# Raw attention outputs of chunks 0 and 1 in a buffer of their own, and four early steps of VectorE and ScalarE in another order

## The chip, the cores and the metric

The kernel runs on one core of a Trainium2 chip. The metric is the device time of one execution in microseconds (us); lower is better. TensorE (PE) does the matmuls, VectorE (DVE) and ScalarE (ACT) the elementwise work, GpSimd (POOL) a few small steps, and SyncE (SP) issues nearly all DMAs. Each engine works through its own list of instructions in order; semaphores make one engine wait for another or for a DMA.

## The reference

```python
# retention over 768 tokens, 4 batches, 8 heads, head size 64
for t in range(S):
    state = gamma * state + outer(k[:, :, t], v[:, :, t])
    y[:, :, t] = scale * (q[:, :, t] @ state)
x = y.transpose(0, 2, 1, 3).reshape(3072, 512)
# then a gated layer
h = x @ w_in                  # 512 -> 2048
g = h * sigmoid(h)
out = g @ w_out               # 2048 -> 512
```

All is float32 at the interface. The weights arrive in 64-bit form and are turned into float32 words on the chip.

## The kernel before, in words

**Tiling.** The 768 tokens are cut into 6 chunks of 128. A *unit* is one chunk of one batch, so there are 24 units; unit n is chunk n // 4 of batch n % 4. `w_in` is cut into 16 slices of 128 columns. A *product* (c, f) is chunk c of all four batches (512 rows) times slice f. Each operand of a large matmul is split into three parts (high, low and third), so a product is 8 matmuls into PSUM tile `ha` (4 with the high part of x, then 4 with the low part) and 4 into `hb` (third part). After all products a second stage multiplies g by `w_out`.

**One unit in attention.** `stage_t` (L436, L438) turns k and q over on TensorE (tiles kp and qp) and ScalarE copies them out (kt, qt). `scale_k`, written K (L398), scales k. TensorE then computes sc (L452, L462). `steps_a`, written A three times, makes am on VectorE (L470), mid (L476 on ScalarE in chunk 0, L478 on VectorE later) and the new state (L482). `scale_q`, written Q (L403), scales qt. `stage_y` computes y in PSUM in three groups (L501): the scores part from am, the first half of the states part from qt with mid and state, and the second half behind a fence on GpSimd (L377). The PSUM tile of y has one buffer, so the scores of unit n + 1 wait until unit n's y has been copied out.

**From y to x.** `steps_y`, written X four times, takes y on. The first step is the *raw copy* on ScalarE (L539) from PSUM to SBUF, for chunks up to `LATE` = 2. The second is the high part of x on ScalarE (L552), then the low part (L555) and the third part (L558), both on VectorE. The raw copy goes to a tile of pool `hpool`, tag "hs", which has three buffers. The same three buffers hold the results g of the products: `close_steps` copies `ha` out (L655, ScalarE), subtracts `hb` (L660, VectorE), applies silu (L665, ScalarE), and `put_g` stores the tile with a DMA on SyncE (L671). A buffer comes free when its put has landed or its last reader is done.

**Weights.** `early_slice`, written W, turns slices 0 to 2 of `w_in` into float32 (L196 on ScalarE, L199 to L217 on VectorE) and splits them (L120, L126 on ScalarE; L123, L128 on VectorE), one step at each call.

**What sets the order.** TensorE's order is that of the program throughout. Until L874 the order of SyncE, VectorE, ScalarE and GpSimd is also the written one: the lines from L763 to L873 are a schedule made by hand, in which units 0 to 7, the weight slices 0 to 2 and the first four products (P(0), P(1), P(2) and P(NF), which are products 0 to 2 of chunk 0 and product 0 of chunk 1) interleave. After that a scheduler orders these engines from given constraints. The part that the change touches lies wholly in the first 70 us. The tag "wq" in pool `wpool` holds 24 KB per partition: first chunk 2's x (units 8 to 11), later four weight slices.

Of the kernel before, what the change touches and what calls it, by code (L numbers as in the profile page):

```python
# [13 lines left out]
FP32 = mybir.dt.float32  # L14
# [19 lines left out]
def kernel(  # L34
# [28 lines left out]
    nc = tc.nc  # L63
    B, H, S, D = q.shape
    DM, DF = moe_w_in.shape
    C = 128
    NC = S // C
    HP = H // 2
    KIN = DM // 128
# [11 lines left out]
    def pool(name, bufs, **kw):  # L81
        return ctx.enter_context(tc.tile_pool(name=name, bufs=bufs, **kw))

    dram = pool("dram", 1, space=bass.MemoryType.DRAM)
    wpool = pool("wpool", 1)
# [12 lines left out]
    y_dram = [dram.tile([128, KIN, C], FP32, tag=f"y{b}", name=f"yd_{b}") for b in range(B)]  # L98
# [136 lines left out]
    def early_slice(i):  # L235

        out = []
        yield from convert_steps(i, out)
        yield
        steps = split_steps(i, out[0], "wi", scale, w_sb, None)  # L240
        next(steps)
        yield from steps
# [186 lines left out]
    def stage_t(n):  # L429

        for name, to, bufs, src, tp in (
                ("kt", kt, 2, kqv["k"][n], turn(f"kp_{n}")),
                ("qt", qt, 3, kqv["q"].pop(n), banks("q", f"qp_{n}", 1)[:, 0])):
            tp = tp.rearrange("p (a t) -> p a t", a=HP)
            for a in range(HP):
                nc.tensor.transpose(tp[:, a, :], src[:, 2 * a : 2 * a + 2, :], ident)  # L436
            to[n] = one.tile([128, HP, C], FP32, tag=name, name=f"{name}_{n}", bufs=bufs)
            evac[:] = [nc.scalar.copy(out=to[n], in_=tp).ins]  # L438
# [88 lines left out]
    def finish_y(n, yp):  # L527
        list(steps_y(n, yp))

    def steps_y(n, yp):  # L530
        c, b = units[n]
        if b == 0:
            p, tag = (wpool, "wq") if c == LATE else (xpool, "xt")
            xt[c] = p.tile([128, 3, KIN, NT], FP32R, tag=tag, name=f"xt_{c}")
        raw = None
        if c <= LATE:

            raw = hpool.tile([128, KIN, C], FP32, tag="hs", name=f"ys_{n}")
            nc.scalar.copy(out=raw.rearrange("p a (o t) -> p o a t", o=2), in_=yp)  # L539
            if c == LATE:  # L540
                nc.sync.dma_start(out=y_dram[b], in_=raw)
        yield from split_x(c, b, yp, raw)

    def split_x(c, b, y, raw):
        yield
        x = [xt[c][:, i, :, ts(b, C)] for i in range(3)]
        if raw is None:
            src = y
            xh, xl = (t.rearrange("p a (o t) -> p o a t", o=2) for t in x[:2])
        else:  # L550
            (xh, xl), src = x[:2], raw
        held[:] = [nc.scalar.activation(out=xh, in_=src, func=AF.Copy, scale=HALF).ins]  # L552

        def lower():
            nc.vector.tensor_tensor(out=xl, in0=src, in1=xh.bitcast(FP32), op=ALU.subtract)  # L555

        def third():
            nc.vector.scalar_tensor_tensor(out=x[2], in0=x[1].bitcast(FP32),  # L558
                                           scalar=-1.0 / EPS, in1=x[0].bitcast(FP32),
                                           op0=ALU.mult, op1=ALU.add)  # L560

        def rest():
            lower()
            third()

        if c > LATE or c == LATE and y is not None:
            behind_next.append(rest)
            return
        yield
        lower()  # L570
        yield
        third()

    LATE = 2
# [148 lines left out]
    sa, ys, asteps, ysteps = {}, {}, {}, {}  # L723

    def T(n):
        stage_t(n)

    def SC(n):
        sa[n] = sc, sums = score_tile(n)
        stage_s(n, sums)  # L730
        stage_a(n, sc)
        asteps[n] = steps_a(n, sc, sums)

    def A(n):
        next(asteps[n], None)

    def YA(n):
        ys[n] = stage_y(n)
        ys[n][0]()
        ys[n][1](0)  # L740

    def YB(n):
        ys[n][1](1)
        ysteps[n] = steps_y(n, ys[n][2])

    def X(n):
        next(ysteps[n], None)
# [3 lines left out]
    def W(i, times=1):  # L751
        if i not in slices:
            slices[i] = early_slice(i)
        for _ in range(times):
            next(slices[i], None)

    def loads(n):
        for name in "kqv":
            load(name, n)

    K, Q = scale_k, scale_q
# [16 lines left out]
    W(0), X(0)  # L778
    W(0), W(0)
    YA(1), SC(2)  # L780
    A(2), A(2), Q(2), A(2)
    YB(1), X(1), X(1)
    T(3), K(3)
    X(1), X(1)
    YA(2), YB(2), X(2)
# [1 line left out]
    X(2), W(1), W(1)  # L787
    X(2), X(2)
    YA(3), YB(3), X(3), X(3)
    W(1)  # L790
    T(4), K(4)
    X(3), X(3)
    W(1), W(1), W(1)
    loads(EARLY - 2), loads(EARLY - 1)
    closing = {}

# [17 lines left out]
    put_g(0)  # L814
    W(1)
    T(5)
    A(4), K(5), A(4), Q(4), A(4)
    W(1), W(1)
    YA(4), SC(5), YB(4)
    loads(EARLY)  # L820
# [116 lines left out]
    for c in range(NC):  # L937
# [9 lines left out]
        for f in range(NF):  # L947
            n = c * NF + f
# [3 lines left out]
            t = ready[n]  # L952
# [17 lines left out]
        for b in range(B):  # L970
            oa, ob = acc[b]
            o = one.tile([128, DM], FP32, tag=("kt", "qt")[b % 2], name=f"o_{c}_{b}",
                         bufs=(2, 3)[b % 2])
# [8 lines left out]
            n = 2 if b == B - 1 else 1  # L982
# [36 lines left out]
```

## Time and profile before

| | us |
|---|---|
| median of 4 runs | 624.86 |
| the four runs | 623.62, 623.82, 625.89, 626.32 |
| the profiled execution | 627.74 |
| its span (first to last instruction) | 625.8 |
| TensorE busy in the span | 606.1 |
| VectorE, ScalarE, GpSimd busy | 423.3, 312.5, 22.1 |
| DMA | 107.31 MB, mean 171 GB/s |

Each engine's share of the span is its busy time by 625.8. The "waits" views give, for an engine, the time it stood idle, the line that it stood at, and the line that released it (`<-`). In a timeline each row has the start in us, the length in us, the engine, the line and the tiles; a bracket gives the idle time before it and what ended it. "PEclk" is the granted share of TensorE's clock. In these rows the buffer numbers of tiles are left out, so units have to be told apart by their order. The times of matmuls are modelled at their ends, and 32 rows of small matmuls that overlap are merged into one.

### The profile page before, as it was taken

Reading aid. Unit: us, or ns where it says so; the run is one execution under the profiler, and the core shown is the slowest. Engines: PE = TensorE matmul, PEld = TensorE weight load, DVE = VectorE, ACT = ScalarE, POOL = GpSimd, SP = SyncE. Lnnn points to the kernel's source line nnn. Section 1 sums busy time; section 2 is a strip of 40 time slices with the busy share of each in tenths; the row PEclk is TensorE's granted clock in tenths of the full one; section 3 lists DMA queues with packets and bytes.
Section 4 is the critical chain, followed back from the end, with each engine's and each line's share of the span. In section 5 each row is a group of like instructions: output and inputs, shape, how many; then the busy total and the mean of one; then the engine's idle time right before and its main releaser. Section 6 shows DMA issues by size and latency. Waiting matters only on the chain.

```text
span 625.8 us, 13496 instructions
## 1 busy us (share of the span) xinstructions
PE 606.1 (97%) x5384; PEld 499.9 (80%) x5384; DVE 423.3 (68%) x731; ACT 312.5 (50%) x595; POOL 22.1 (4%) x79
## 2 busy tenths in 40 slices
PE   6897999999999999999999999999999999999997
PEld 5776787888888887788788888888888888888886
DVE  4897898898879886777599793553635544554631
ACT  6676787666655565666588651312312221312311
POOL 3000000000000211111000000000000000000000
PEclk9898999999999999999999999999999999999999
DMA  9997787545568898999867543342533523342301
GB/s 190 217 228 173 195 242 207 192 151 190 191 172 242 222 263 206 246 246 266 289 222 255 198 134 101 118 151 68 169 102 101 168 86 116 135 130 77 130 1 67
DMA packets 137998, 107.31 MB, mean 171 GB/s; under 512 B 94800, under 2 KB 103248, under 8 KB 137936
## 3 DMA queue, kind: packets, MB, share of 16 engines
q1 hardware_dynamic: 135056, 101.21, 57.0%
q10 hardware_dynamic: 2880, 5.24, 2.3%
q8 instruction: 42, 0.69, 0.4%
q14 instruction: 20, 0.16, 0.1%
HBM read 66.06 MB, written 36.70 MB: 164 GB/s over the span
## 4 chain that ended last, share of the span: by engine, by line
PE 79%; DMA 1%; ACT 1%; SPq 1%; issue 0%; DVE 0%; DVEq 0%; POOLq 0%
PE ha L645 22%; PE o L959 20%; PE oa L959 14%; PE hb L645 11%; PE ob L959 7%; PE y L501 2%; PE sc L462 1%; DMA qw<-qp 1%; DMA kw<-kp 1%; PE sc L452 1%; SPq L671 0%; PE o L967 0%; ACT kt L426 0%; PE oa L967 0%; ACT qt L426 0%
## 5 line engine op out<-in xcount | busy, mean ns | idle before, releaser
L645 PE MATMUL ha<-xt,wi 128*128 128x512 f32 x768 | 194.3, 395 | 0.8 <-ACT wi L126 0.4
L645 PEld LDWEIGHTS ha<-xt,wi 128*128 128x128 f32 x768 | 142.5, 188 | 32.8 <-ACT wi L126 1.2
L959 PE MATMUL o<-wo,gs 128*128 128x512 f32 x564 | 143.2, 389 | 0.0
L959 PEld LDWEIGHTS o<-wo,gs 128*128 128x128 f32 x564 | 105.9, 188 | 21.9
L712 DVE TENSOR_TENSOR gs<-gr,gs 128x512 fp32r<-128x512 f32 x96 | 62.2, 686 | 90.3 <-ACT gs L710 90.3
L710 ACT ACTIVATE gs<-gr 128x512 fp32r<-128x512 f32 x96 | 53.6, 621 | 134.2 <-issue 131.8
L959 PE MATMUL oa<-wo,gs 128*128 128x512 f32 x376 | 115.8, 389 | 0.0
L645 PE MATMUL hb<-xt,wi 128*128 128x512 f32 x384 | 103.1, 390 | 0.6 <-DVE g L660 0.6
L660 DVE TENSOR_TENSOR g<-g,hb 128x512 f32<-128x512 f32 x96 | 65.6, 684 | 44.7 <-ACT g L655 30.4
L645 PEld LDWEIGHTS hb<-xt,wi 128*128 128x128 f32 x384 | 71.8, 188 | 16.6 <-DVE g L660 1.0
L665 ACT ACTIVATE g<-g 128x512 f32<-128x512 f32 x96 | 60.3, 628 | 46.0 <-DVE g L660 46.0
L959 PEld LDWEIGHTS oa<-wo,gs 128*128 128x128 f32 x376 | 70.6, 188 | 14.7
L655 ACT ACTIVATE g<-ha 128x512 f32<-128x512 f32 x96 | 57.0, 593 | 33.6 <-PE ha L645 14.3
L959 PE MATMUL ob<-wo,gs 128*128 128x512 f32 x188 | 73.7, 392 | 0.0
L713 DVE SCALAR_TENSOR_TENSOR gs<-gs 128x512 fp32r<-128x512 f32 x96 | 62.1, 684 | 0.0
L959 PEld LDWEIGHTS ob<-wo,gs 128*128 128x128 f32 x188 | 35.3, 188 | 8.7 <-DVE o L977 1.6
L196 ACT ACTIVATE ca<-wf 128x512 f32<-128x512 f32 x32 | 21.3, 667 | 7.5 <-DVE cw L217 6.2
L470 DVE TENSOR_TENSOR am<-sc,decay 128x512 f32<-128x512 f32 x24 | 16.5, 687 | 10.9 <-PE sc L462 10.8
L212 DVE SCALAR_TENSOR_TENSOR ca<-wf,ca 128x512 f32<-128x512 uint32 x32 | 22.7, 710 | 0.5
L976 ACT ACTIVATE o<-o 128x512 f32<-128x512 f32 x10 | 6.0, 600 | 33.4 <-PE o L959 33.0
L206 DVE SCALAR_TENSOR_TENSOR cs<-ca,cs 128x512 uint32<-128x512 uint32 x32 | 22.1, 691 | 0.8
L501 PE MATMUL y<-qt,mid 64*64 64x64 f32 x384 | 20.6, 226 | 1.0 <-POOL token L377 0.8
(92 smaller groups left out, 564.4 us busy)
## 6 DMA issues: line engine op xcount, KB each, us to landing
gd<-g SPq DMA_DIRECT2D x96, 256.0 KB, 3.1
gr<-gd SPq DMA_DIRECT2D x96, 256.0 KB, 2.7
wf<-in_moe_w_out_dram SPq DMA_DIRECT2D x16, 512.0 KB, 4.5
out_dram<-o ACTq DMA_DIRECT2D x20, 256.0 KB, 2.1
wf<-in_moe_w_in_dram SPq DMA_DIRECT2D x16, 256.0 KB, 4.2
wf<-in_moe_w_in_dram SPq DMA_DIRECT2D x32, 128.0 KB, 4.1
kf<-in_k_dram SPq DMA_DIRECT2D x16, 256.0 KB, 5.4
qf<-in_q_dram SPq DMA_DIRECT2D x16, 256.0 KB, 3.6
```

Source lines behind the costliest of these rows:

```text
L196: nc.scalar.activation(out=a.bitcast(FP32), in_=hi.bitcast(FP32), func=AF.Abs, scale=65536.0)
L206: nc.vector.scalar_tensor_tensor(out=s, in0=a, scalar=3, in1=s, op0=ALU.logical_shift_left, op1=ALU.bitwise_or)
L212: nc.vector.scalar_tensor_tensor(out=p.bitcast(FP32), in0=lo, scalar=2.0 ** -52, in1=p.bitcast(FP32), op0=ALU.mult, op1=ALU.mult)
L501: i = nc.tensor.matmul(yp[ts(e, D), o, a, :], lhsT=lhsT, rhs=rhs, start=(e, o) not in started, stop=True, skip_group_check=True).ins
L645: nc.tensor.matmul(hb if i == 2 else ha, lhsT=w_sb[f][:, i, ts(kk, 128)], rhs=xt[c][:, i, kk, :], start=kk == 0 and i != 1, stop=kk == KIN ...
L655: copied[:] = [nc.scalar.activation(out=hs, in_=ha, func=AF.Copy, scale=ONE_E).ins]
L660: taken_out[:] = [nc.vector.tensor_tensor(out=hs, in0=hs, in1=hb, op=ALU.subtract).ins]
L665: nc.scalar.activation(out=hs, in_=hs, func=AF.Silu)
L710: nc.scalar.activation(out=t[:, 0, :], in_=g, func=AF.Copy, scale=HALF)
L712: nc.vector.tensor_tensor(out=t[:, 1, :], in0=g, in1=high, op=ALU.subtract)
L713: nc.vector.scalar_tensor_tensor(out=t[:, 2, :], in0=t[:, 1, :].bitcast(FP32), scalar=-1.0 / EPS, in1=high, op0=ALU.mult, op1=ALU.add)
L959: nc.tensor.matmul(o, lhsT=g, rhs=wo[f][:, i, :], start=f == 0 and i != 1, stop=f == NF - 1 and i != 0)
```

## The change

Raw copies of units 0 to 7 no longer go to "hs". One tile `ys` of 8 raw outputs (16 KB per partition) is taken from tag "wq" at unit 0, and unit n writes and reads its part n. Chunk 2's x is the next tile under that tag, so its first write must come after the last read of `ys`. Units 8 to 11 still take their raw copy to "hs" and store it.

The other part rewrites the written order at four places:

- unit 1's raw copy (first X(1)) goes on ScalarE ahead of mid of unit 2 (second A(2));
- for unit 3, the low and third parts go on VectorE ahead of K(4), and the fourth step of weight slice 1 (L206) goes ahead of both;
- K(5) goes behind mid of unit 4 and Q(4).

No instruction is added or removed, and the orders on TensorE, SyncE and GpSimd are the same.

```diff
+    raws = []
+
     def steps_y(n, yp):
...
-        if c <= LATE:
-
+        if c < LATE:
+            if n == 0:
+                raws.append(wpool.tile([128, LATE * B, KIN, C], FP32, tag="wq", name="ys"))
+            raw = raws[0][:, n]
+            nc.scalar.copy(out=raw.rearrange("p a (o t) -> p o a t", o=2), in_=yp)
+        elif c == LATE:
             raw = hpool.tile([128, KIN, C], FP32, tag="hs", name=f"ys_{n}")
             nc.scalar.copy(out=raw.rearrange("p a (o t) -> p o a t", o=2), in_=yp)
-            if c == LATE:
-                nc.sync.dma_start(out=y_dram[b], in_=raw)
+            nc.sync.dma_start(out=y_dram[b], in_=raw)
         yield from split_x(c, b, yp, raw)
...
     YA(1), SC(2)
-    A(2), A(2), Q(2), A(2)
-    YB(1), X(1), X(1)
+    A(2)
+    YB(1), X(1)
+    A(2), Q(2), A(2)
+    X(1)
     T(3), K(3)
...
     YA(3), YB(3), X(3), X(3)
-    W(1)
-    T(4), K(4)
+    W(1), W(1)
+    T(4)
     X(3), X(3)
-    W(1), W(1), W(1)
+    K(4)
+    W(1), W(1)
...
     T(5)
-    A(4), K(5), A(4), Q(4), A(4)
+    A(4), A(4), Q(4), K(5), A(4)
     W(1), W(1)
```

## The prediction

> **What bounds the kernel now.** The page's first part, the clock row of its second and the head of its chain come first:
>
> ```profile
> PE 606.1 (97%) x5384; PEld 499.9 (80%) x5384; DVE 423.3 (68%) x731; ACT 312.5 (50%) x595; POOL 22.1 (4%) x79
> ...
> PEclk9898999999999999999999999999999999999999
> ...
> PE 79%; DMA 1%; ACT 1%; SPq 1%; issue 0%; DVE 0%; DVEq 0%; POOLq 0%
> ```
>
> TensorE sets the end: it is busy for 97% of the span. Its idle time lies at the start, where the clock row also dips twice. A table by stretches gives TensorE 125.56 busy of the 126 us from 74 to 200, and nothing in the change touches what comes later. So an edit is worth the time by which TensorE reaches the dense part (from about 59 us) earlier, and nothing else. The waits before 140 us on TensorE, then before 110 us on ScalarE:
>
> ```profile
> PE y L501 <- ACT ys L539: 4.8, 2, 3.9
> PE kp L436 <- POOL step L342: 4.2, 1, 4.2
> PE y L501 <- DVE am L470: 1.7, 2, 0.9
> ```
> ```profile
> ACT ys L539 <- DMA gd<-g: 4.8, 1, 4.8
> ```
>
> 4.2 us is the start. The largest is 3.9 us behind a raw copy (L539), and that copy waits 4.8 us for a put of g to land. The timeline from 46 to 64 us has the place:
>
> ```profile
> 48.38 0.54 SPq L671 DMA_DIRECT2D gd<-g  x1
> 48.42 0.60 ACT L655 ACTIVATE g<-ha 128x512 f32<-128x512 f32 x1 [0.57 <-PE y L501]
> ...
> 53.78 0.59 ACT L539 COPY ys<-y 128x512 f32<-128x512 f32 x1 [4.76 <-DMA gd<-g]
> ...
> 54.42 1.13 PE L501 MATMUL y<-am,kqv 64*64 64x64 f32 x32 [3.87 <-ACT ys L539]
> ...
> 57.66 0.69 DVE L470 TENSOR_TENSOR am<-sc,decay 128x512 f32<-128x512 f32 x1 [3.83 <-PE sc L462]
> ```
>
> g_0_1's put was issued at 48.38 and landed 5.3 us later. Unit 6's raw copy takes over its buffer (the three "hs" buffers turn round), so ScalarE stands 4.76 us, TensorE 3.87 (unit 7's scores need PSUM y) and VectorE 3.83. Last, the clock, by stretches (length, PE, PEld, DVE, ACT, POOL busy, PEclk, DMA share, GB/s):
>
> ```profile
> 23.22:26.63 3.41, 2.08 (x98) 1.70 (x88) 2.52 (x7) 1.95 (x4) 0.09 (x1) 1.00 0.77 172
> 26.63:30.05 3.42, 3.42 (x18) 3.08 (x19) 2.73 (x5) 2.66 (x6) 0.00 (x0) 0.50 0.98 236
> ...
> 50.53:53.94 3.41, 0.02 (x1) 0.00 (x0) 3.27 (x6) 0.16 (x1) 0.00 (x0) 1.00 0.76 182
> 53.94:57.35 3.41, 2.93 (x108) 2.93 (x112) 0.00 (x0) 3.41 (x9) 0.09 (x1) 0.50 0.37 85
> ```
>
> After each slack stretch TensorE gets half its clock for 3.4 us.
>
> **Part 1: the buffer of their own.** No instruction is added or removed. The listing of both programs by engine shows TensorE, SyncE and GpSimd in the same order. The raw copies of units 5, 6 and 7 lose their waits for g_0_0's put, g_0_1's put and unit 5's readers; only unit 6's cost anything. Worked on from there:
> - ScalarE ends g_0_2's copy at 49.02. Unit 6's matmuls end at 49.52, so its raw copy runs 49.56 to 50.15, and unit 7's am ends at 50.05. TensorE is in unit 8's transposes until 50.55, so unit 7's scores start there, not at 54.42.
> - Then VectorE is what is late: from am 7 (49.36) it has continuous work to 53.84. Unit 8's sc would be done by about 52.8 at full clock (0.69 scores, states after qt 7 at 50.98, sc after K(8) at 51.59 in two overlapping groups of 0.69 and 0.65). So am 8 starts at 53.77, as rows on VectorE overlap by 0.07, not at 57.66: **3.89 us**.
> - The first product of chunk 1 needs unit 7's lower part (59.60 to 60.29), 1.94 us after am 8 in the same VectorE order, so it too comes 3.89 us earlier. ScalarE's xt of unit 7 comes 4.2 earlier and is no bound.
>
> Waits that come in. The turn of "hs" shifts: unit 8's raw copy (69.50) now waits for g_0_2's put (issued 57.05, landed after 2.9), and g_1_1's copy (66.79) for g_0_1's, landed at 53.7. Behind them on ScalarE stand unit 8's xt, wi of slice 3 and g_1_2's copy, for which TensorE would wait. The cover is 9.5 and 13.1 us against a longest landing of 6.2: nothing. Chunk 2's x, in "wq" after the raw outputs, is first written at 70.13; their last reader ends at 60.29, 9.8 us before: nothing. If either cover went, the price would be a stall like the one above.
>
> **Part 2: the four reorderings.**
> - Unit 1's raw copy before mid 2. mid 2 waits for am 2 (ends 20.32), the copy only for unit 1's matmuls (end 19.35). It runs 19.39 to 19.98, not 20.62 to 21.21. Unit 2's scores then wait for am 2 plus 0.14 (as am 3's end at 24.77 to 24.91): 20.46, not 21.27, **0.81 us**. mid 2 doesn't move. From the scores to sc 3's end is 2.72 now; K(3) (21.78) and qt 3 (22.21) are there before their use. am 3 is at 23.27, unit 3's scores at 24.10, their last part at 25.31.
> - The conversion step L206 and unit 3's lower and third before K(4). Now unit 3's last part takes 1.02 us at half clock (26.12 to 27.14); at 25.31 the clock is full and it takes 0.40. Raw copy 25.75 to 26.34, xt high 26.38 to 27.01. VectorE's third of unit 2 ends at 26.48, L202 at 26.82, L206 at 27.43; lower 27.36 to 28.05, third 28.08 to 28.77, against 30.30 now. K(4), L209, L212 end at 30.36; sc 4 needs K(4) (29.4) only after the product. The product is 12 matmuls of 0.227 (1.82 for 8), 0.454 at half clock, and 0.16 to the end; hb now ends at 32.33 and VectorE takes it at 32.44. From 27.05: with the half clock still from 26.63 to 30.05, 6.6 matmuls in that time and 5.4 after it: 31.44, **0.89 us** earlier. With full clock hb ends at 30.08 and VectorE is free at 30.36: **2.08 us**. This contains the 0.81.
> - mid 4 and Q(4) before K(5). Unit 4's states wait for Q(4) (0.84 us at 35.91) and come 0.6 earlier; but sc 5 needs K(5), which now ends 3.44 us after the L660 row. With 0.1 to TensorE that is 3.55, against 3.85 now (36.29 - 32.44): **0.30 us**.
> - From there to 50.5 TensorE is busy throughout or waits for VectorE's chain from am 5, which shifts too, so the gain is kept.
>
> What is late next is loading: SyncE issues without a pause until about 49 us and doesn't come earlier. Slice 2's w lands at about 33.5 and is read now at 35.53; unit 6's q lands at 35.0, is read at 38.11; unit 10's q (issued 50.58 when unit 8's buffer is free, landing 56.4) is read at 62.73. Minus 1.2 to 2.4, or minus 5 to 6 for the last, they still just fit.
>
> **Sum against the profiled execution** (627.74 us: span 625.8 and 1.9 around it): 3.89 + 0.30 + 0.89 = 5.08, or with 2.08, 6.27. It ran 2.9 above the median. Without the two half-clock stretches before would have lost less: am 8 at 56.76 (0.90 earlier) and the L660 row at 31.06 (1.38 earlier), 2.3 together; the gain is then 6.27 - 2.28 = 3.99. The four runs shown fall into pairs at 623.72 and 626.11, 2.39 apart. That the pairs are these two cases is a guess from the sizes, but both lead to one place: 623.72 - 3.99 = 619.7 and 626.11 - 6.27 = 619.8; where one half-clock stretch stays, 621.0. I take **620.0**, 4.9 below the median.
>
> [...]
>
> **Rivals.**
> - Only the wait pays; the early moves are eaten by loads (33 to 36 us) or a half-clock stretch that moves along. For: SyncE issues back to back, DMA share about 1.0. Against: TensorE shows no wait for DMA there. Gain 2.99 to 3.89: 621.4.
> - The wait changes hands to a transfer: unit 10's q, 2.84 us in issue. If it lands 3 us late, TensorE stands in its transposes and 2 us are left: 623.0. Against: the DMA engines are nearly idle from 54 to 57.
> - More: the freed stretch also removes small waits that I left in place: 618.0.
> - Slower: unit 8's copy waits for g_0_2's put. TensorE needs PSUM y for unit 9's scores at 73.13, so the copy has 3.0 us of cover beyond 69.50; to lose 4.9 + 3.1 the put must land some 23 us after issue (57.05 to 80.5). Then 628.5. The longest landing seen is 6.2.
> - That the edit doesn't do what it says is excluded by the listing: the waits are gone from those three copies.
>
> **Numbers.** Forecast 620.0: 0.62 (its own range 618.6 to 621.4). Only the wait: 0.20. Transfer: 0.09. More: 0.06. Slower: 0.03. 0.5% is 3.1 us (621.7), about what a measurement of this kernel can tell from no change. Faster: 0.62 + 0.06 + 0.13 of the second = 0.81; same 0.07 + 0.09 = 0.16; slower 0.03. The range 617.8 to 622.2 takes in the forecast, nearly all of the second and part of the fourth.
>
> **What would show it.** Right: no "ys L539 <- DMA" wait; unit 7's scores directly after unit 8's transposes; no half clock behind it; first chunk-1 product 5 to 6 us earlier; VectorE without a gap from am 7 to am 8; unit 2's scores waiting for am. Wrong: TensorE waiting for DMA at kp or qp, or ScalarE at ca; a half-clock stretch inside the dense part; a new wait at unit 8's copy.

## The result, and the profile after

The changed kernel takes 622.02 us (median of 35 runs, 620.12 to 625.63); before takes 624.97 in 54 runs. The ratio is 0.9951 with a 95% interval of 0.9941 to 0.9962: 3.0 us less, where 4.9 were forecast. The measured time lies in the range, 2.0 us above the forecast and 0.2 below the upper end. The prediction gave 0.81 to a gain of more than 0.5%; the measured 0.49% falls just short of it.

The profiled execution of the changed kernel took 621.75 us, near its median; the one of before was 2.8 above its own. So the 5.8 us between the spans of the two profiles must not be taken for the effect. The same lines of the page:

```profile
PE 604.5 (98%) x5384; PEld 498.9 (80%) x5384; DVE 423.5 (68%) x731; ACT 312.6 (50%) x595; POOL 22.0 (4%) x79
...
PEclk9899999999999999999999999999999999999999
...
PE 80%; DMA 1%; ACT 1%; SPq 0%; issue 0%; DVE 0%; DVEq 0%; POOLq 0%
```

One of the two clock dips is gone. TensorE's waits before 110 us:

```profile
PE kp L436 <- POOL step L342: 4.1, 1, 4.1
PE y L501 <- DVE am L470: 1.7, 2, 0.9
PE y L501 <- POOL token L377: 1.5, 3, 0.9
PE sc L452 <- PE y L501: 0.5, 1, 0.5
PE sc L452 <- DVE state L482: 0.5, 1, 0.5
PE y L501 <- issue: 0.5, 1, 0.5
```

The 4.8 us behind the raw copies have left the list. Four entries are new or longer. Three of them are where the reorderings' gain went: 0.9 at a fence, 0.5 at "issue" and 0.5 at sc 5. The fourth, 0.5 at unit 8's sc (51.87 us), lies behind the old wait, where VectorE is now what is late. The place of the old wait in the timeline:

```profile
49.26 0.69 DVE L470 TENSOR_TENSOR am<-sc,decay 128x512 f32<-128x512 f32 x1 [0.30 <-PE sc L462]
...
49.51 0.59 ACT L542 COPY ys<-y 128x512 f32<-128x512 f32 x1 [1.26 <-PE y L501]
...
50.38 0.69 PE L501 MATMUL y<-am,kqv 64*64 64x64 f32 x32
...
53.66 0.68 DVE L470 TENSOR_TENSOR am<-sc,decay 128x512 f32<-128x512 f32 x1
```

Unit 6's raw copy (now L542) waits only for its own matmuls, unit 7's scores follow unit 8's transposes, and VectorE's am 8 starts at 53.66. The clock around the two stretches that had fallen to half:

```profile
22.96:26.37 3.41, 1.74 (x94) 1.62 (x87) 2.47 (x6) 1.98 (x4) 0.09 (x1) 1.00 0.73 163
26.37:29.78 3.41, 3.22 (x18) 2.93 (x18) 2.89 (x5) 2.28 (x5) 0.00 (x0) 0.50 0.97 226
50.40:53.80 3.40, 2.93 (x134) 2.72 (x134) 3.37 (x7) 3.25 (x9) 0.09 (x1) 1.00 0.86 202
```

The later one is gone, the earlier one is still there, and TensorE is less busy ahead of it (1.74 us of 3.41) than it was in the profile of before (2.08).

Starts of the same matmuls in the two profiles, by their place in TensorE's order, before and after: sc 4 32.26 and 32.17, first product of slice 1 38.47 and 38.38, unit 7's scores 54.42 and 50.38, the last four matmuls of chunk 1's first product 61.37 and 57.37. Of the 0.09 at the first two, 0.08 was there from the first matmul on. So **all of the profile's early gain, 4.0 us, comes at the wait, and the reorderings brought nothing**. The other 1.8 of the 5.8 us arise later: about 0.6 by 146 us, and 1.0 between 229 and 310 us. That last stretch took 81.0 us in this profile of before, 80.0 in the one after, and 80.0 and 79.2 in the profiles of e3 and e2 below, so it varies without the change.

### The profile page after: what moved, and what is told of

It is laid out like the page before. It is cut to its first block, busy times and chain, and to the rows that moved or that the text cites. A ratio compares the mean times of both kernels' runs of the same rounds, so it can differ in the third digit from the quotient of the medians.

```text
span 620.0 us, 13494 instructions
## 1 busy us (share of the span) xinstructions
PE 604.5 (98%) x5384; PEld 498.9 (80%) x5384; DVE 423.5 (68%) x731; ACT 312.6 (50%) x595; POOL 22.0 (4%) x79
## 4 chain that ended last, share of the span: by engine, by line
PE 80%; DMA 1%; ACT 1%; SPq 0%; issue 0%; DVE 0%; DVEq 0%; POOLq 0%
PE ha L650 23%; PE o L967 21%; PE oa L967 14%; PE hb L650 11%; PE ob L967 7%; PE y L501 2%; DMA qw<-qp 1%; PE sc L462 1%; PE sc L452 1%; ACT qt L426 0%; PE o L975 0%; SPq L676 0%; ACT kt L426 0%; PE oa L975 0%; PE qp L436 0%
## 5 line engine op out<-in xcount | busy, mean ns | idle before, releaser
L206 DVE SCALAR_TENSOR_TENSOR cs<-ca,cs 128x512 uint32<-128x512 uint32 x32 | 22.1, 691 | 0.9
L501 PE MATMUL y<-qt,mid 64*64 64x64 f32 x384 | 20.3, 225 | 1.5 <-POOL token L377 1.5
```

Source lines behind the costliest of these rows:

```text
L206: nc.vector.scalar_tensor_tensor(out=s, in0=a, scalar=3, in1=s, op0=ALU.logical_shift_left, op1=ALU.bitwise_or)
L501: i = nc.tensor.matmul(yp[ts(e, D), o, a, :], lhsT=lhsT, rhs=rhs, start=(e, o) not in started, stop=True, skip_group_check=True).ins
```

## The experiments

Theory A: the buffer is the whole gain. Theory B, the prediction's: the reorderings carry 1.2 to 2.4 us of it.

**The two parts apart, and the wait's price (e1 to e4).** e1 is the changed kernel with the old order:

```diff
-    A(2)
-    YB(1), X(1)
-    A(2), Q(2), A(2)
-    X(1)
+    A(2), A(2), Q(2), A(2)
+    YB(1), X(1), X(1)
...
-    A(4), A(4), Q(4), K(5), A(4)
+    A(4), K(5), A(4), Q(4), A(4)
```

> The raw outputs in a buffer of their own, the order of the steps as before. Theory A (the buffer is the whole gain; the reorderings move nothing that TensorE waits for): as the changed kernel, about 622.0 us, 2 to 4 us below before, unit 7's scores at about 50.4 us directly behind unit 8's transposes. Theory B (my prediction: the reorderings carry about 1.2 to 2.4 us of the gain): 623.2 to 624.0, 1 to 2 us above the changed kernel.

Measured: 620.59 us (6 runs), ratio to before 0.993 (0.9909 to 0.995). That is 1.4 us below the changed kernel, where A expected the same time and B 1 to 2 us more. The two were timed in different rounds.

e2 is the kernel before with the new order (the same lines the other way round):

> The four reorderings alone, the raw outputs in the three shared buffers. Theory A: no change from before, within 0.5 us of 625.0, and the 3.9 us wait of unit 7's scores stays, since the put of g_0_1 goes out when SyncE comes to it and not when the result is ready. Theory B: 1.0 to 2.4 us below before, with the products of the first 50 us that much earlier.

Measured: 624.61 us (11 runs), ratio 0.9985 (0.9969 to 1.000). In its profile TensorE waits 4.5 us for the raw copy. Its sc 4 starts at 30.84 against 30.73 in e3's profile, and slice 1's first product at 37.05 against 37.06: in these profiles the reorderings move nothing by then. B's earlier products fall. The time alone does not exclude B's 1.0 us: before took 625.59 in the same rounds, 1.0 more, and the interval of the ratio reaches from nothing to 1.9 us. Whether the 0.15% is anything stays open.

e3 is the kernel before, unchanged:

> The kernel before, once more, for a second profile. If the half-clock stretch behind the 3.9 us wait depends on how the clock's windows of 3.41 us lie (theory: they are not tied to the kernel), it is missing or lies elsewhere in this profile, and the span from unit 7's scores to the first product of chunk 1 is then about 0.9 us shorter than the 4.8 us of the first profile. If it belongs to the wait itself, it is there again at the same place.

Measured: 625.25 us. There is no half clock at 26 us; behind the wait there are two stretches of it, earlier than in the first profile (length, engines' busy time, PEclk, DMA share, GB/s):

```profile
47.60:51.01 3.41, 1.53 (x44) 1.23 (x36) 3.10 (x7) 0.00 (x0) 0.00 (x0) 1.00 0.87 258
51.01:54.43 3.42, 1.16 (x44) 1.16 (x48) 1.38 (x3) 1.80 (x5) 0.00 (x0) 0.50 0.97 217
54.43:57.84 3.41, 3.41 (x101) 3.29 (x94) 1.23 (x2) 2.72 (x8) 0.09 (x1) 0.50 0.24 83
```

The windows do lie differently (half clock from 51.01 here, from 53.94 in the first profile), but unit 7's scores to the first product take 5.1 us, not 0.9 less than 4.8: windows that are 45% and 34% busy are each followed by 3.4 us at half clock. In both profiles half clock follows the wait; in the other three profiles with the old wait (e2, e9, e11) it runs from about 51.6 to 58.5 us too.

e4 is the kernel before with one load moved on SyncE:

```diff
-    load_w(4)
     W(2)
     CL(1), CL(1)
...
     put_g(0)
+    load_w(4)
     T(7)
```

> The kernel before with one move on SyncE alone: the load of weight slice 4 goes behind the put of g_0_1, so the put goes out at about 46 us instead of 48.4. If the wait of unit 6's raw copy is for that put's landing, it ends about 2.4 us earlier (at about 51.4 instead of 53.8) and TensorE's wait falls from 3.9 to about 1.5 us; total 1 to 2.4 us below before. If the copy waits for something else (its own matmuls, VectorE), the wait stays at 3.9 us and the time at 625.

Measured: 621.74 us (4 runs), ratio 0.9941 (0.9921 to 0.9961). The put goes out at 45.42 and the wait ends early, as expected; the gain of 3.7 us is larger than expected:

```profile
45.42 1.73 SPq L671 DMA_DIRECT2D gd<-g  x1
...
50.05 0.58 ACT L539 COPY ys<-y 128x512 f32<-128x512 f32 x1 [2.37 <-DMA gd<-g]
...
50.69 0.69 PE L501 MATMUL y<-am,kqv 64*64 64x64 f32 x32 [1.52 <-ACT ys L539]
```

TensorE still waits 1.5 us, but no half clock follows (windows 55% and 68% busy). The wait is 2.4 us shorter and the time 3.7 less; that the rest is the half clock behind the wait, which the prediction reckoned at 0.90 us, is my estimate. One moved load gets as far as the whole change.

**The four combinations side by side (e9 to e12).** In these and the rest, q and k of units 17 to 23 are turned over by TensorE as for earlier units, not by DMA (after 200 us); the added transposes cost about 5 us.

> The kernel before, with q and k of units 17 to 23 turned over by TensorE as for the units ahead of them, and not by DMA; nothing before about 240 us is touched. It serves as the common ground for the next three, in the same rounds. Both theories: some 5 to 12 us above before (7 units of 8 transposes of about 1.2 us together per unit, by the rows of kp and qp), the wait of unit 7's scores still 3.9 us or more.

> e9 with the raw outputs in their own buffer and the old order. Theory A (the buffer is the whole gain): 3 to 4.5 us below e9. Theory B (my prediction: half of it or less): 3 to 3.9 us below e9 and 1 to 2.4 us above e12.

> e9 with the four reorderings alone. Theory A: within 0.6 us of e9. Theory B: 1.0 to 2.4 us below e9.

> e9 with the whole change. Theory A: within 0.6 us of e10, 3 to 4.5 us below e9. Theory B: 4 to 6 us below e9. Theory C (the reorderings cost something on top of the buffer): 0.8 us or more above e10.

| | median us (runs) | ratio to before, interval | mean granted clock | executions at full clock |
|---|---|---|---|---|
| e9, neither | 630.23 (6) | 1.0090, 1.0074 to 1.0106 | 0.9952 | 0 |
| e10, buffer | 626.23 (12) | 1.0025, 1.0012 to 1.0039 | 0.9979 | 6 |
| e11, order | 629.26 (6) | 1.0082, 1.0065 to 1.0099 | 0.9948 | 0 |
| e12, both | 627.59 (11) | 1.0044, 1.0028 to 1.0061 | 0.9963 | 3 |

"At full clock" is a granted clock of 0.999 or more over the execution. The buffer alone gives 4.0 us here and 5.0 in e1; the whole change gives 2.6 and 3.0. A is right on where the gain is: it comes with the buffer, and B's 1 to 2.4 us in favour of e12 are not there. The reorderings on top look like a cost of 1.4 us in both pairs, which is theory C, but the intervals of e10 and e12 meet, so by the time alone C isn't settled. The order without the buffer is about 1.0 below e9, as e2 was below before: outside A's 0.6, at the lower end of B, and within the noise, as the intervals of e11 and e9 meet. In their profiles, whose clock rises within 0.1 us of each other, sc 4 starts at 30.55 in e11 against 30.61 in e9, and slice 1's first product at 36.76 against 36.97, so at most 0.2 us is gained by then.

**Which step costs (e15).** e12 with unit 1's raw copy behind mid 2 again:

```diff
-    A(2)
-    YB(1), X(1)
-    A(2), Q(2), A(2)
-    X(1)
+    A(2), A(2), Q(2), A(2)
+    YB(1), X(1), X(1)
```

> e12 with unit 1's raw copy back behind mid 2; the other reorderings and the buffer stay. Theory D (that step is what costs: it gathers TensorE's idle time in the stretch from 23 to 26.5 us, so more executions fall to half clock behind it): mean granted clock as in e10 (0.998, most executions at 0.999 or 1.0), time 0.8 to 1.4 us below e12's 627.6. Theory A2 (the difference between e10 and e12 is chance): clock and time between the two, 626.2 to 627.6, with no order among the three.

Measured: 626.96 us (12 runs), ratio 1.0019 (1.0000 to 1.0038), mean clock 0.9979, 7 of 12 at full clock. The clock is as in e10. The time lies halfway between e10 and e12, but those ran in other rounds, in which before took 624.91 and not 625.80 as in e15's. Against before in its own rounds e15 is 1.2 us above, e10 1.3 and e12 2.7, which is about what theory D expects; the intervals of e15 and e12 still meet. Over the kernels with the buffer and the loads as they were, 14 of 46 executions run at full clock where that step is in (the change itself 11 of 35, e12 3 of 11) and 20 of 36 where it is not (e1 6 of 6, e10 6 of 12, e15 7 of 12, and e16 below 1 of 6). Such a difference would come by chance in about 3 cases of 100 (Fisher's test). But most of these kernels differ in more than that step; for e12 and e15, which differ in it alone, it would come by chance in about 1 case of 5. So neither the clock nor the time shows more than a tendency that this step costs something.

**Why TensorE gained nothing from that step (e13, e14, e16).** In the changed kernel unit 2's scores do start early, and then stop inside:

```profile
20.40 0.68 PE L501 MATMUL y<-am,kqv 64*64 64x64 f32 x26
21.54 0.34 PE L501 MATMUL y<-am,kqv 64*64 64x64 f32 x6 [0.46 <-issue]
```

Nothing in the program separates the 26th score from the 27th. The next such stop comes 127 matmuls later, behind a fence that alone cost 0.28 us before:

```profile
26.56 0.69 PE L501 MATMUL y<-qt,mid 64*64 64x64 f32 x8 [0.95 <-POOL token L377]
```

Before has a trace of it at the same matmul, in the weight loads:

```profile
26.12 1.02 PE L501 MATMUL y<-qt,mid 64*64 64x64 f32 x8 [0.28 <-POOL token L377]
...
26.52 0.44 PEld L501 LDWEIGHTS y<-qt,mid 64*64 64x64 f32 x7 [0.27 <-issue]
```

The page of the changed kernel lists the packets of queue 8, which it calls an instruction queue (packets, MB, share of the DMA engines):

```profile
q8 instruction: 42, 0.69, 0.5%
```

In the trace each of the 42 packets has 16384 B. If all of them are for TensorE's 2 x 5384 matmuls and weight loads, 0.69 MB is 64 B for each and a packet 256 of them: 127 matmuls with their weight loads and two more, and 127 matmuls is also the distance of the two stops. So, by this estimate, one packet looks like one block of TensorE's instructions, and the stops like block boundaries. The test changes what the blocks compete with, e13 in e12 and e14 in e10:

```diff
+            rows = src[b].rearrange("h (t e) d -> (h t) (e d)", e=H)
+            nc.sync.dma_start(out=t.rearrange("t h d -> t (h d)"), in_=rows[ds(c * C, C)])
```

> e12 (the whole change) with the q, k and v loads of units 0 to 7 made of 2 KB rows that lie together instead of 256 B rows; it computes on other values, the bytes and all other instructions are the same. Theory F (unit 2's scores stop after 26 of 32 matmuls because TensorE's next 16 KB of instructions come late, behind the packets of the loads): with an eighth of the packets the block comes sooner; the pauses of 0.46 and 0.95 us at that matmul and 127 matmuls later go or fall under 0.2 us. Rival (the pauses belong to the program: a semaphore, the PSUM tile): same places, same lengths.

> e10 (the buffer alone) with the same loads of 2 KB rows; other values are computed. Theory F: unit 2's scores wait about 0.9 us for unit 1's raw copy and nothing stops inside them; with the instruction blocks out of the way the reordering of that copy is worth 0.5 to 0.9 us at unit 3's scores between e13 and e14. Rival: no difference above 0.2 us there.

Measured: 630.07 us (4 runs) and 630.76 (10 runs). Each set against before in its own rounds, that is 1.6 and 3.6 us above e12 and e10; for e13 the intervals meet. The pauses didn't go; most grew. e14, where none was expected (four lines added make L501 L505 and L542 L546):

```profile
20.38 0.68 PE L505 MATMUL y<-am,kqv 64*64 64x64 f32 x26 [0.70 <-ACT ys L546]
22.06 0.34 PE L505 MATMUL y<-am,kqv 64*64 64x64 f32 x6 [1.00 <-issue]
```

and e13, at the second place:

```profile
27.97 0.69 PE L505 MATMUL y<-qt,mid 64*64 64x64 f32 x8 [2.05 <-issue]
```

So with the loads in fewer, larger packets the block came later, against my expectation. With the order of TensorE's instructions untouched, e13 stops for 0.74 and 2.05 us, where the changed kernel stopped for 0.46 and 0.95 and e12 for nothing and 0.68. So the length is not set by the program: it varies between profiles of the same instructions, and it grew with the other loads. In e14 the second place shows only the fence's 0.28 us. Unit 3's scores start at 24.99 and 25.81, the difference expected, but e14 was at half clock from 23.44 on, so the pair says nothing about the step itself.

The trace also has the start and end of each packet of queue 8. The times in us, for some of the stops:

| stop ahead of matmul | block before it begins | packet starts | packet ends | matmul starts |
|---|---|---|---|---|
| 347th, changed kernel | 17.14 | 18.96 | 20.13 | 21.54 |
| 474th, e12 | 20.65 | 22.55 | 23.85 | 25.35 |
| 474th, e13 | 21.85 | 25.36 | 26.39 | 27.97 |
| 1107th, e12 | 46.88 | 48.97 | 49.96 | 51.40 |
| 1107th, e15 | 48.99 | 52.61 | 53.60 | 55.12 |

At these three places no profile has the block's first matmul sooner than 1.3 us after the end of its packet, and wherever TensorE stops there, it goes on 1.3 to 1.7 us after it. What differs is how long the packet takes to start after the block before has begun: 1.8 to 3.6 us in these rows, 1.6 us more in e13 than in e12 at the same place. In e14 the packet at the second place also starts later than in e10 (3.4 us after the block before against 2.1), but TensorE was late itself, so no stop shows. By these times the stops are waits for the instructions.

e16 puts ten transposes of the identity ahead of unit 0 in e10:

```diff
+    warm = banks("q", "warm", 1)[:, 0]
+    for i in range(10):
+        nc.tensor.transpose(warm[:, ts(i % 4, 128)], ident, ident)
     T(0), K(0)
```

> e10 with ten transposes of the identity on TensorE while it waits for unit 0's k (about 1.4 to 4.1 us); their result is not used. If TensorE's clock rises by what it did in the 3.4 us windows before, full clock comes at about 6 to 9 us instead of 16 to 17.5 in most executions, and unit 2's scores start up to 1.5 us earlier, as in e1's profile where full clock came at 7.5 us: 0.5 to 1.5 us below e10's 626.2. If the clock's rise doesn't hang on the work before, no change.

Measured: 630.45 us (6 runs), ratio 1.0069 (1.0046 to 1.0092): each set against before in its own rounds, 3.3 us above e10. Full clock came at 16.2 us as usual, although the window from 2.6 to 6.0 was now 84% busy: the hope failed. But e16 shows the blocks. With ten matmuls added ahead, the stop comes ten matmuls earlier in the work, at the last of unit 3's scores and not behind the fence after them:

```profile
24.74 0.69 PE L501 MATMUL y<-am,kqv 64*64 64x64 f32 x31 [0.92 <-DVE am L470]
26.09 0.21 PE L501 MATMUL y<-am,kqv 64*64 64x64 f32 x1 [0.65 <-issue]
```

Counted from TensorE's first matmul, it is at the 474th here and in e1, whose early instructions are those of e10 (0.27 us, at 25.43). So this stop kept its place in the instruction stream and not in the work. A block boundary five blocks on, inside unit 8's sc, gives pauses of 0.3 us in e1 and e10, 0.6 in e12, and in e15, whose profile is of its slowest execution, 2.2:

```profile
55.12 0.59 PE L462 MATMUL sc<-qt,kt 64*64 64x64 f32 x10 [2.20 <-issue]
```

Before, TensorE stood for the raw copy just ahead of that place, and no pause shows there, nor does one in the profile of the changed kernel. Where it shows, part of the wait removed comes back as this one. In e15's profile half clock follows from 54.17 to 61.00, and the last four matmuls of chunk 1's first product start at 61.13, hardly earlier than the 61.37 of before.

## Why the prediction was right or wrong

- **What bounds it, and the wait (Part 1): right, place and size.** Unit 7's scores were forecast for 50.55, am 8 for 53.77 and unit 7's lower part for 55.71; they came at 50.38, 53.66 and 55.59. The price of 3.0 to 3.9 fits the mean difference of e10 and e9, 3.75, and of e1 and before (4.15 over its own rounds). The shifted waits cost nothing, as said.
- **Unit 1's raw copy, 0.81 us: wrong.** In the profile after, the scores start 0.87 earlier and lose 0.64 of it at the block boundary, and the next boundary (26.56 after, 26.52 before) takes the rest. In e12's profile the first boundary costs nothing and the second 0.40, so the loss is not the same in every execution. The prediction read the timeline for engines and DMAs and took TensorE's instructions as always present. The row for this was in the timeline of before: "issue" at unit 3's last part, at 26.52.
- **Unit 3's lower and third before K(4): wrong.** The 0.89 to 2.08 us contained the 0.81 and let the product start at 27.05, with unit 3's last part at 25.31 and at full clock. That part came at 26.56, at half clock, and the product at 28.80 (before: 26.12 and 28.69). The third part held nothing up: TensorE shows no wait inside that product in any profile, with half clock or full; its 12 matmuls took 3.64 us before and 3.45 after, at half clock up to 30.05 and 29.78. The end of hb at full clock, given as 30.08, comes to 29.93 by the sum's own terms, which changes nothing, as VectorE's 30.36 was the bound.
- **K(5) behind Q(4), 0.30 us: wrong, by a wait overlooked.** Unit 4's states do come 0.69 earlier, but sc 5 goes to the PSUM tile that state 4 (L482) reads last, and state 4 has kept its place: it ends at 36.10, sc 5 starts at 36.21. VectorE has the same five steps to do before sc 5 in either order. The two rows before, then after:

```profile
35.78 0.41 DVE L482 TENSOR_TENSOR state<-mid,sc 128x256 f32<-128x256 f32 x1
...
36.29 0.69 PE L452 MATMUL sc<-kqv 64*64 64x64 f32 x32
```
```profile
35.69 0.41 DVE L482 TENSOR_TENSOR state<-mid,sc 128x256 f32<-128x256 f32 x1
...
36.21 0.69 PE L452 MATMUL sc<-kqv 64*64 64x64 f32 x32 [0.52 <-PE y L501]
```

- **The sum and the base.** That the two pairs of runs are the two clock cases was a guess, and 62 executions of before in the experiments' rounds don't bear it out: none has full clock, 9 have a mean of 0.996 or more (median 623.74), the rest have less (median 625.6). In the changed kernel 11 of 35 have full clock (620.76), 15 have 0.997 (622.02), the figure of its profile, where one stretch of 3.4 us is at half clock, and the 9 that lose more have medians of 623.2 to 623.6. At like clock (623.74 against 622.02) the gain is 1.7 us; by these groups the rest of the 3.0 is executions that fall to half clock less often. That is a reckoning and not a test: where the half-clock stretches of these executions lay is not on record. The prediction counted the clock in one profile and not how often it falls.
- **The rivals.** The one with 0.20, "only the wait pays" (621.4), came true, and only half by the mechanism that it named: the half-clock stretch at 26 us did stay, but the profiles of e2 and e11 have none there and gain at most 0.2 us by slice 1's first product. What ate the early moves in them was, by their waits, late blocks of instructions (in e2's profile 0.7 us at a fence and 0.2 at "issue") and a wait that had been overlooked (0.5 ahead of L452), and the third part had held nothing up. That the measured 622.02 lies inside the range is in part luck: the range held because it was drawn to reach there, by 0.2 us. The transfer (unit 10's q) never became a wait.
- **The clock and the instructions.** The clock fell, or stayed low, not only after windows that were 1% and 61% busy, as in the profile of before, but also after some of 34% and 45% (e3) and 51% (the changed kernel). Over the first 66 us of all 14 profiles, half clock followed every full-clock window under 52% busy and none above 62%; between them it went either way (52% in e1, 60% in e12 and 55% in e4 were spared; 52% in e14, 54% in e16 and 61% in before and e15 were not). That is what these profiles had, and not a bound that a run tested. The stops at the block boundaries, which the prediction didn't count, took up to 2.2 us (e15, at 55.12).

What stays open: whether the reorderings cost time beyond the tendency, whether without the buffer they gain the 1.0 us that e2 and e11 hint at, and why the blocks came later with the loads in larger packets. The buffer with the old order (e1, 620.59) has the best median of the unaltered kernels, but its interval and that of the change (0.9909 to 0.995, 0.9941 to 0.9962) meet.

## What to carry to other kernels

Price a wait of TensorE with the clock behind it: in e4 2.4 us less waiting came with 3.7 less time, and its profile has no half clock behind the 1.5 us of waiting that are left (windows 55% and 68% busy). Before counting a step moved ahead as a gain, look at what else the next instruction needs: the buffer that it overwrites, and its own arrival (here "issue" in the middle of a uniform group, for 0.46 us, and the next stop 127 matmuls on). Compare medians, not two profiles, when single executions of one kernel spread by 5 us, and set kernels that ran in different rounds against one that ran in both: before itself differed by 0.9 us between the rounds of e10 and of e15.

## What the runs showed that was not expected

- TensorE stood for 0.2 to 2.2 us at the 347th, about the 474th and the 1107th matmul of these programs, in e16 and e1 at the 474th with different work there. Queue 8 moved 42 packets of 16384 B, by the estimate above 256 of TensorE's instructions each, and TensorE went on 1.3 to 1.7 us after the end of one. In some profiles no stop shows at the same place (e12 at the 347th).
- With the same 256 KB loads in 2 KB rows instead of 256 B rows, most of those stops were longer (0.68 us in e12, 2.05 in e13), and the programs 1.6 and 3.6 us slower (e13 against e12, e14 against e10).
- Full clock came at 16.1 to 17.6 us in most profiles and at 7.5 and 7.7 in those of e1 and e10, where the 3.4 us window before was 95 to 96% busy by the rows; in the profile of before it came at 16.39, behind a window that was 100% busy. Windows 84% (e16) to 92% busy (9.57 to 12.98 in before) were not followed by it there. Later in the profile of before, one of 86% was (53.94 to 57.35).
